# S4 convolution beside a gated FFN: channel halves, channel pairs, and last reads in three parts

## The chip, the cores and the metric

One core of a Trainium2 chip runs the whole program. The metric is the device time of one execution in microseconds; the lower the better. The kernel before the change took 326.91 us (median of 3 runs, 326.82 to 329.02).

## What is computed

The input is `u`, 2048 rows by 640 channels in bf16. Two branches read it and are mixed by a gate per row. The core of the reference:

```python
logdA = exp(log_dt)[:, None] * (A_re + 1j * A_im)            # 640 x 128
K  = einsum("dn,dnl,dn->dl", C, exp(logdA[:, :, None] * l), dt * B).real   # 640 x 2048
a  = irfft(rfft(pad(u.T)) * rfft(pad(K)))[:, :2048].T + u * Dskip
b  = (gelu(u @ w_gate) * (u @ w_up)) @ w_down                # 640 -> 1728 -> 640
g  = sigmoid((u * gate_w).sum(-1))
out = g * a + (1 - g) * b
```

So there is a long convolution per channel with a kernel K that must first be generated from 128 complex states per channel, and a feed-forward network with 1728 hidden units.

## The kernel before, in words

**Generating K.** A time index is split as one of 32 coarse steps times one of 20 fine steps (`X2`), centred at 124, so K at a channel is a product of two small tables summed over the 128 states, which lie on the partitions. `kgen(q)` makes the tables for one half `q` of the channels (320 = `W`): `cs1` (32 coarse steps) and `cs2` (20 fine steps), each with a cosine and a sine plane. ScalarE writes the magnitudes (`exps1`, L599: 32 activations of 320 elements for each half, one for each sign and step; `exps2`, L627: 20 more) and the sines of the phases (L589); VectorE writes the phases (L580, L582, L584) and the products (L613, L614, L619, L631, L637). `contract(h)` then multiplies on TensorE (L650): four neighbouring channels ("quads") share one matmul, with a 128-column stationary tile (32 steps x 4 channels) and 80 moving columns (20 steps x 4 channels), 80 quads by two planes, so 160 matmuls for each half. Only the quarter of the result in which the channels agree is used. Seven evictions (128x960 and one 128x640, L247 or L243) copy it to `kst`, two groups of selecting matmuls (`pick`, L661) take the wanted quarter, and four DMAs write it to DRAM (`dS`). A first row of K (L669, L672) is made in `contract` too.

**Transforms.** The convolution is done in two stages of matmuls with a small matrix (`WA`, then `TB`), through DRAM between the stages. `ua` (L719) is stage A of u: 16 phases, written to `dU`. `gathers(h)` reads rows of `dS` into the tile `Kl` with 18 DMAs, into runs of 16, 16, 32 and 64 neighbouring partitions, and `stageA(h)` (L780) writes the stage-A result for one half to `dKA`, which holds both halves side by side (rows of 640 channels, of which a half fills 640-byte pieces). Stage B is `stageB` (L807): for each of eight blocks `c` of 4 columns, four groups of matmuls over 64x64 tiles, each followed by an eviction. `u_spec(c)` gives the spectrum `U[c]`; `swap` copies `U[c]` with neighbouring partitions exchanged into `Us` (two DMAs). `mix(c)` loads all 640 channels of `dKA`, runs stage B on them, multiplies `U` and `Us` by the result on VectorE (L826, L827: 128x2560 each), does the inverse stage (L834) and writes `dY`. Only four `Us` buffers exist, so the swaps for c = 4 to 7 come between the mixes.

**Finish.** `finish` reads `dY` back in eight tiles (L847, 640 KB each, all 128 partitions, four buffers in a ring), runs two groups of matmuls for each (L854), combines each with the FFN result on VectorE (L859), and writes the output (L863).

**FFN.** `ffn(0)` and `ffn(1)` are two halves of the rows: 14 gate groups (L500, gelu on ScalarE at L504) and 13 up groups (L520, product on VectorE at L524) each. `downs(0)` and `downs(1)` are eight groups each of 28 matmuls (L548) with one eviction (L245 or L249). `downs(0)` must be through before the hidden units of `ffn(1)` take its buffers.

**The order.** Each operation is added as a numbered step. The list `ORDER` holds one number v for each: step v // 20, engine v % 20 // 4 (PE, DVE, ACT, POOL, SP), PSUM bank pair v % 4. `emit` issues the steps in exactly this order, so every engine's queue is written out by hand, and all DMAs go through SP's queue. The durations and ranks given with each step were input of the planner that made the list; they do nothing at run time. The order of TensorE that matters here: two `downs(0)` groups and 8 of the `ua` phases, then the contraction of half 0, the rest of `downs(0)`, `ffn(1)` with the last `ua` phases between, the contraction of half 1 at 182 us, the stage B of u, stage A of K half 1, and from 238 us on the eight `downs(1)` groups laid singly between stage B of K and the inverse stage. The last of them, `down1.7`, stands before the last inverse groups; after those nothing but the finish is left.

Of the kernel before, what the change touches and what calls it, by code (L numbers as in the profile page):

```python
# [8 lines left out]
ALU = mybir.AluOpType  # L9
# [18 lines left out]
    336 1392 652 276 12 296 356 436 616 476 636 948 516 24 376 416 316 456 496 964 556 536 44 596 1468 576 224 676  # L28
    696 64 896 936 856 2740 1448 876 396 984 6316 796 1484 816 916 836 1408 716 736 1544 2981 2836 776 756 1064 1428
    2862 3076 1004 1024 1044 4383 2956 2768 1124 1084 1104 2888 10580 10604 3008 4404 2782 10636 1508 3020 2804 2856  # L30
    1568 1604 2903 3096 248 3044 88 3101 2976 4428 1664 2602 1148 6320 3196 6348 2624 2924 1168 6362 2656 3220 6436
    6388 1524 1188 6416 3128 3463 3316 3248 4444 3142 1584 3556 3488 1628 3261 3216 3164 1204 6440 1688 3336 6483
    3822 3284 6556 6464 6508 1644 3501 1228 3916 6536 3848 3340 3576 1244 1264 4183 1284 3368 3436 3524 1704 6562
    4208 4276 6600 3581 6676 6588 6628 6656 3703 1724 3608 3676 1304 3622 3728 3796 3940 3696 1324 3644 1348 4061
    4036 104 3968 6683 1364 4156 6722 1944 6796 4088 3860 6748 2004 6708 1748 6776 3981 3936 3884 3382 4056 1828
    1764 4004 1788 4223 3456 3404 1868 1804 4300 4296 1908 1844 4244 128 1924 3741 4376 1884 1968 144 6802 3816 6843
    6916 3764 6828 1984 6868 168 6896 4101 2064 2028 4176 4328 6922 2124 6963 7036 6988 6948 4344 2088 7016 184 4124
    2044 7043 208 7082 7068 4460 2184 7156 7108 2148 7136 2104 2164 2208 9464 7161 7203 4488 4742 7276 7188 2224
    7228 7256 9524 2480 4768 2321 2504 2443 2344 2242 2464 2360 2264 2281 2384 2403 2304 7322 2424 9728 7280 4661
    7396 7304 7344 9768 9744 7376 9808 2523 9784 2560 4684 4502 2588 2544 9848 9824 2716 2736 9408 2696 9864 2676  # L40
    7401 4524 7440 4703 7516 7424 9888 7464 8276 8296 8236 9448 9904 7496 8316 8436 8336 4542 4724 8456 8536 8576
    9388 8416 8356 8396 8496 8476 8556 7521 4564 7560 9428 8256 4583 7636 7584 8376 8516 7544 7616 9488 4622 4604
    9548 9584 7680 7641 4648 9504 4783 7756 7668 7708 7736 4902 4808 4876 9644 5021 9608 4996 9564 7760 5116 7803
    7876 7824 7788 9668 9924 5260 7856 5048 4823 5356 9984 4928 7921 4896 7948 4844 7882 7996 7908 4941 5288 9684
    7976 5142 5016 4964 10008 8003 5236 8040 9624 5061 8116 8068 5136 10104 8028 5300 9948 8096 5383 5376 5324 5168
    10044 8160 5476 5408 8122 8188 5503 5084 8148 8216 9964 5420 5528 5596 9704 10068 5742 10024 5496 5444 8621
    10128 5836 8583 10164 5180 8608 11176 11356 8648 5623 10144 5256 5768 8676 5204 5861 5716 5648 10084 10188 5782
    5956 5540 5804 5856 5888 11536 10204 8723 5616 8682 5564 8708 10221 8748 10262 8776 10244 10300 10284 10343
    10324 10381 10364 8822 10404 8780 8848 10423 8808 10462 8876 10444 11221 11260 10488 11244 11183 11288 11302
    11716 11204 11328 11541 11360 11568 11384 11402 12636 11663 11428 12616 8881 11684 8920 8908 11582 8944 10503  # L50
    11608 11621 10524 10540 11648 12076 8976 5902 10568 12696 12716 10656 10716 10676 11721 11763 5924 11800 11748
    10696 5976 11828 11841 11784 12256 11442 11868 11480 11896 11504 11468 12203 12161 12736 12228 12184 12756 12082
    12120 12656 12108 9023 12144 12676 8981 9048 5982 9004 9076 6080 13076 6008 13036 13056 13116 13096 6163 12976
    6108 13016 12996 12956 12936 12261 12816 12342 6188 12380 12284 12896 12916 12368 12404 12023 12776 12301 12048
    12856 6122 12324 12836 12876 12796 6076 11900 11943 6144 11981 11928 12436 11968 9080 12004 9122 9108 6203 9144
    9176 5661 6224 13120 5684 5736 13162 13148 13363 13188 13260 13384 13321 13288 13222 13216 13344 12443 13248
    12480 12468 12504 12562 13316 9181 13416 12588 12523 9204 6020 12548 13422 6044 13461 13448 13523 13548 13562
    13484 6240 13588 13516 13616 13663 6268 11052 13621 13684 9222 9248 13644 9276 13763 6284 13722 13716 13788
# [11 lines left out]
    17124 17276 17436 17296 17576 17716 17481 17443 17504 17996 17464 17302 17340 17556 17324 17536 17364 17856  # L70
    17581 17623 17396 17604 17416 17644 18136 17722 17760 17744 17676 18276 17784 17696 18041 18003 18064 17816
    17836 18024 18116 17862 18096 17900 17884 17924 17956 18141 17976 18183 18164 18204 18282 18236 18320 18256
    18304 18344 18396 18376
""".split()]


# [64 lines left out]
def kernel(  # L141
# [90 lines left out]
    def evac(n, p, dst, src, r=(), w=(), rank=3.0, act=True, dve=True, scale=None, **k):  # L232
        e = {}
        if act:
            e["ACT"] = an(n)
# [722 lines left out]
```

## Time and profile before

| | us | share of the span |
|---|---|---|
| median of 3 runs | 326.91 | |
| the profiled execution, its own time | 327.61 | |
| its span, first to last instruction | 325.8 | |
| PE (matmuls) busy | 266.1 | 82% |
| PEld (weight loads) busy | 146.7 | 45% |
| DVE (VectorE) busy | 246.3 | 76% |
| ACT (ScalarE) busy | 223.6 | 69% |
| mean granted TensorE clock | 0.922 of full | |

How to read it: an engine's "busy" is the time in which at least one of its instructions ran; weight loads run beside matmuls. A "group" is all instructions of one line, engine and shape, with its busy time and the mean time of one. The "chain of work" goes back from the last instruction, at each step to what released it. A "window" row gives, for a stretch of the span, its length, then the busy time and count for PE, PEld, DVE, ACT and POOL, then the granted clock, the busy share of the 16 DMA engines and the GB/s moved.

### The profile page before, as it was taken

Reading aid. Unit: us, or ns where it says so; the run is one execution under the profiler, and the core shown is the slowest. Engines: PE = TensorE matmul, PEld = TensorE weight load, DVE = VectorE, ACT = ScalarE, POOL = GpSimd, SP = SyncE. Lnnn points to the kernel's source line nnn. Section 1 sums busy time; section 2 is a strip of 40 time slices with the busy share of each in tenths; the row PEclk is TensorE's granted clock in tenths of the full one; section 3 lists DMA queues with packets and bytes.
Section 4 is the critical chain, followed back from the end, with each engine's and each line's share of the span. In section 5 each row is a group of like instructions: output and inputs, shape, how many; then the busy total and the mean of one; then the engine's idle time right before and its main releaser. Section 6 shows DMA issues by size and latency. Waiting matters only on the chain.

```text
span 325.8 us, 5490 instructions
## 1 busy us (share of the span) xinstructions
PE 266.1 (82%) x2112; PEld 146.7 (45%) x2126; DVE 246.3 (76%) x332; ACT 223.6 (69%) x307; POOL 5.3 (2%) x18
## 2 busy tenths in 40 slices
PE   0799999897796999979899987985998889993452
PEld 0254444443366677534344743432465456551220
DVE  4687999999999963799996977254363899982464
ACT  4998997699995599998989576525471386671000
POOL 3000000000000000000000000000110000000000
PEclk9989999999797999999999997999899799998555
DMA  6993344332321144433437659979366569934997
GB/s 171 394 331 104 121 140 125 100 103 81 125 76 42 62 123 130 143 123 120 141 100 240 188 192 291 341 163 260 115 204 221 181 240 330 344 141 163 368 353 245
DMA packets 47519, 60.57 MB, mean 186 GB/s; under 512 B 4419, under 2 KB 41862, under 8 KB 47494
## 3 DMA queue, kind: packets, MB, share of 16 engines
q1 hardware_dynamic: 47494, 60.23, 57.3%
q8 instruction: 16, 0.26, 0.3%
q14 instruction: 9, 0.07, 0.1%
HBM read 35.80 MB, written 19.17 MB: 169 GB/s over the span
## 4 chain that ended last, share of the span: by engine, by line
PE 36%; ACT 22%; DVE 18%; DMA 15%; issue 5%; SPq 3%; DVEq 0%; ACTq 0%
PE ps L548 13%; PE ps L520 8%; PE ps L500 7%; ACT arena L243 6%; ACT arena L589 5%; DVE arena L247 5%; DMA dKA<-arena 4%; ACT arena L599 4%; DMA arena<-dY 3%; DMA arena<-dU 3%; ACT arena L504 3%; DMA arena<-dKA 2%; DVE arena L859 2%; PE ps L650 2%; PE ps L807 2%
## 5 line engine op out<-in xcount | busy, mean ns | idle before, releaser
L243 ACT CAST arena<-ps 128x640 bf16<-128x640 f32 x111 | 70.6, 702 | 38.1 <-PE ps L807 15.7
L500 PE MATMUL ps<-arena 128*128 128x512 bf16 x276 | 66.5, 392 | 13.0 <-DMA arena<-in_u_T_dram 9.2
L247 DVE CAST arena<-ps 128x640 bf16<-128x640 f32 (+2 forms) x67 | 56.2, 881 | 20.1 <-PE ps L807 10.4
L520 PE MATMUL ps<-arena 128*128 128x512 bf16 x250 | 63.1, 401 | 4.2 <-DVE arena L524 1.9
L548 PE MATMUL ps<-arena 128*128 128x320 bf16 x448 | 65.0, 305 | 1.0 <-DVE arena L247 0.5
L548 PEld LDWEIGHTS <-arena 128*128 128x128 bf16 x448 | 44.5, 100 | 20.6 <-issue 2.1
L500 PEld LDWEIGHTS <-arena 128*128 128x128 bf16 x280 | 28.0, 100 | 47.9 <-issue 14.1
L520 PEld LDWEIGHTS <-arena 128*128 128x128 bf16 x260 | 26.5, 103 | 37.2 <-issue 9.3
L589 ACT ACTIVATE arena<-arena 128x2560 bf16<-128x2560 int16 x18 | 41.6, 2334 | 0.4 <-DVE arena L637 0.3
L524 DVE TENSOR_TENSOR arena<-ps,arena 128x1024 bf16<-128x1024 f32 x26 | 31.6, 1218 | 13.1 <-PE ps L520 12.9
L504 ACT ACTIVATE arena<-ps 128x1024 bf16<-128x1024 f32 (+1 forms) x28 | 27.7, 1023 | 9.4 <-PE ps L500 9.2
L807 PE MATMUL ps<-arena 64*64 64x320 bf16 x256 | 16.9, 325 | 9.0 <-DMA arena<-dKA 2.8
L599 ACT ACTIVATE arena<-arena 128x320 bf16<-128x320 f32 x64 | 23.3, 455 | 1.0 <-DVE arena L451 1.0
L854 PE MATMUL ps<-arena 128*64 128x320 bf16 x64 | 10.2, 474 | 14.5 <-DMA arena<-dY 14.5
L859 DVE SCALAR_TENSOR_TENSOR arena<-ps,g_f,arena 128x640 bf16<-128x640 f32 x16 | 13.0, 878 | 11.9 <-PE ps L854 11.9
L249 DVE TENSOR_SCALAR arena<-ps,omg 128x640 bf16<-128x640 f32 x10 | 8.8, 883 | 14.9 <-PE ps L548 14.9
L627 ACT ACTIVATE arena<-arena 128x320 bf16<-128x320 f32 x40 | 14.8, 455 | 5.9 <-PE ps L650 5.9
L582 DVE SCALAR_TENSOR_TENSOR arena<-arena 128x320 int32<-128x320 f32 x40 | 16.9, 483 | 0.8 <-ACT arena L589 0.7
L650 PE MATMUL ps<-arena 128*128 128x80 bf16 x320 | 13.5, 212 | 3.8 <-DVE arena L637 2.8
L807 PEld LDWEIGHTS <-arena 64*64 64x64 bf16 x256 | 8.2, 107 | 17.7 <-issue 9.7
L650 PEld LDWEIGHTS <-arena 128*128 128x128 bf16 x320 | 13.3, 107 | 4.6 <-DVE arena L637 3.5
L780 PE MATMUL ps<-arena 128*128 128x320 bf16 x64 | 12.1, 308 | 4.1 <-DMA arena<-dS 2.3
(93 smaller groups left out, 240.8 us busy)
## 6 DMA issues: line engine op xcount, KB each, us to landing
arena<-in_w_gu_dram SPq DMA_DIRECT2D x52, 160.0 KB, 2.2
dU<-arena SPq DMA_DIRECT2D x16, 320.0 KB, 2.3
arena<-dU SPq DMA_DIRECT2D x8, 640.0 KB, 4.7
dKA<-arena SPq DMA_DIRECT2D x16, 320.0 KB, 4.2
arena<-arena SPq DMA_DIRECT2D x16, 320.0 KB, 4.3
arena<-dKA SPq DMA_DIRECT2D x8, 640.0 KB, 6.0
dY<-arena SPq DMA_DIRECT2D x8, 640.0 KB, 6.1
arena<-dY SPq DMA_DIRECT2D x8, 640.0 KB, 5.6
```

The lines of the kernel that those rows point to most:

```text
L243: nc.scalar.copy(out=dst, in_=src(b))
L247: nc.vector.tensor_copy(out=dst, in_=src(b))
L500: nc.tensor.matmul(ps[:, k + j, :], lhsT=Wg[w][:, kt, :], rhs=xT[2 * grp + j][:, kt, :], start=(kt == 0), stop=(kt == NKT - 1))
L504: add({"ACT": an(1024)}, lambda s: nc.scalar.activation(out=HTall[0:p, :, f, :], in_=ps[0:p, plan.bank(g):plan.bank(g) + 2, :], func=ACT.G ...
L520: nc.tensor.matmul(ps[:, k + j, :], lhsT=Wu[w][:, kt, :], rhs=xT[2 * grp + j][:, kt, :], start=(kt == 0), stop=(kt == NKT - 1))
L524: add({"DVE": v1(1024)}, lambda s: nc.vector.tensor_tensor(out=HTall[:, :, f, :], in0=ps[:, plan.bank(u):plan.bank(u) + 2, :], in1=HTall[: ...
L548: nc.tensor.matmul(ps[:, k + h, 0:W], lhsT=HTq[q][:, f, 128 * j:128 * j + 128], rhs=Wd[f][:, W * h:W * h + W], start=(f == 0), stop=(f == ...
L589: ac(an(8 * W), lambda: nc.scalar.activation(out=t[:], in_=ph.bitcast(I16)[:, :, :, 0:32:2], func=ACT.Sin, scale=SIN_SCALE), r=[f"ph{k}"], ...
L599: nc.scalar.activation(out=cs1[:, 1, :, 4 * s:4 * s + 4], in_=quads(aT[:, ds]), func=ACT.Exp, scale=float(sg * (4 + 8 * i)))
L650: nc.tensor.matmul(ps[:, k + i // g, 80 * (i % g):80 * (i % g) + 80], lhsT=cs1[:, x, k0 + i, :], rhs=cs2[:, x, k0 + i, :], start=(x == 0), ...
L807: nc.tensor.matmul(ps[64 * y:64 * y + 64, k + x, 0:W], lhsT=TB[64 * x:64 * x + 64, 0, :], rhs=t[64 * x:64 * x + 64, 2 * a + y, HV[h]], sta ...
L859: add({"DVE": v1(D)}, lambda s, p=p, ph=ph, z=z: nc.vector.scalar_tensor_tensor(out=z, in0=ps[:, plan.bank(p):plan.bank(p) + 2, 0:W], scal ...
```

## The change

Five things are changed together, and the whole order of issue is a new list (952 steps in place of 920).

1. **Channel pairs.** `contract` takes two channels at a time: a 64-column stationary tile (32 steps x 2) and 40 moving columns (20 x 2), 160 pairs by two planes, so 320 matmuls for each half in place of 160. Pairs of the lower and the upper 80 go to PSUM partitions 0 to 63 and 64 to 127. The evictions are three of 128x960 and one of 128x320 for each half in place of seven. All tables have runs of 2 neighbouring channels in place of 4.
2. **Exps of both signs.** A negated copy `aN` of the decay rates is laid beside them, and one activation of 640 elements writes the steps of both signs: 16 in place of 32 for each half.
3. **Products by half.** `dKA` and the products are split by channel half: the load, stage B and products of half 0 (`product(0, c)`) come before stage A of half 1 is done; half 1 follows with the inverse (`product(1, c)`, `inverse`). Loads are 320 KB in 640-byte pieces, writes are 2,560-byte pieces. There are eight `Us` buffers, and the swap follows each `u_spec`.
4. **Rows spread.** The rows of `u` and K are permuted so that the gathers write every 8th, 4th or 2nd partition. About 25 more operations on one column prepare the index tables (`rows`, `last_rows`).
5. **Last reads in three parts.** `dY` is three tensors (blocks c = 0 to 3; 4 and 5; 6 and 7). Each of the eight tiles, which now have a buffer each, is read by three DMAs into every 2nd, 4th and 4th partition.

In the new list TensorE does three `downs(0)` groups and eleven `ua` phases before the contraction of half 0. After the last inverse groups (block c = 5, whose last K stage comes late) stand `down1.5` and `down1.6`, then the finish. SP has the eight reads of blocks 0 to 3 before the writes of blocks 6, 7 and 5, then reads of blocks 6 and 7, then mostly those of 4 and 5, then the outputs.

```diff
-    cs1 = at(O_CS1, [128, 2, 80, 128], BF16, "cs1")
+    cs1 = at(O_CS1, [128, 2, 160, 64], BF16, "cs1")
...
     def exps1(q, i0, n):
...
         def go():
             for i in range(i0, i0 + n):
-                for s, sg in ((15 - i, -1), (16 + i, 1)):
-                    nc.scalar.activation(out=cs1[:, 1, :, 4 * s:4 * s + 4], in_=quads(aT[:, ds]), func=ACT.Exp, scale=float(sg * (4 + 8 * i)))
+                out = c5[:, 1, 15 - i:17 + i:2 * i + 1] if d < 0 else c5[:, 1, 16 + i:(14 - i if i < 15 else None):-2 * i - 1]
+                nc.scalar.activation(out=out, in_=ab, func=ACT.Exp, scale=float(4 + 8 * i))
...
     def contract(h):
-        for k0 in range(0, 80, 12):
-            n = min(12, 80 - k0)
+        for k0 in range(0, 80, 24):
+            n = min(24, 80 - k0)
...
                 for i in range(n):
                     for x in range(2):
-                        nc.tensor.matmul(ps[:, k + i // g, 80 * (i % g):80 * (i % g) + 80], lhsT=cs1[:, x, k0 + i, :],
-                                         rhs=cs2[:, x, k0 + i, :], start=(x == 0), stop=(x == 1))
+                        for y in range(2):
+                            nc.tensor.matmul(ps[64 * y:64 * y + 64, k + i // g, 40 * (i % g):40 * (i % g) + 40],
+                                             lhsT=cs1[:, x, 80 * y + k0 + i, :], rhs=cs2[:, x, 80 * y + k0 + i, :], start=(x == 0), stop=(x == 1))
...
     def kgen(q):
+        ve(v2(W), lambda: nc.vector.tensor_scalar(out=aN[q][:], in0=aT[:, W * q:W * q + W], scalar1=-1.0, scalar2=None, op0=ALU.mult),
+           r=["aT"], w=[f"aN{q}"], rank=RKQ[q] + P["e1"])
...
+        def rows_of(m0):
+            return {0: slice(0, 128, 8), 16: slice(4, 128, 8), 32: slice(2, 128, 4), 64: slice(1, 128, 2)}[m0]
...
-            dst = Kl[m0:m1, phs, :]
+            dst = Kl[rows_of(m0), phs, :]
...
+    def product(h, u, us, kb, bi, c, UK, keys, R):
         (U, un_), (Us, sn), (t, tn) = u, us, kb
+        ks = stageB(loadB(dKA[h][:], W, keys, bi, c, R), (0,), t, tn, R)
+        for x, kx in zip((U, Us), UK):
+            ve(v2(W * CS), lambda x=x: nc.vector.tensor_tensor(out=x[:, :, HV[h]], in0=x[:, :, HV[h]], in1=t, op=ALU.mult), r=ks,
+               w=[k for k in kx if k[2] == h], rank=R - .1)
...
-    def finish(keys, rings, R):
-        for g in range(8):
-            t, nm = rings[g % len(rings)]
-            dma(640, lambda t=t, g=g: nc.sync.dma_start(out=t, in_=dY[:, 4 * g:4 * g + 4, :]), r=keys, w=[nm], rank=R, run=5120)
+    def finish(tiles, R):
+        for q, (p0, st, cs) in enumerate(((0, 2, (0, 1, 2, 3)), (1, 4, (4, 5)), (3, 4, (6, 7)))):
+            for g, (t, nm) in enumerate(tiles):
+                dma(640 // st, lambda t=t, g=g, q=q, p0=p0, st=st: nc.sync.dma_start(out=t[p0:128:st], in_=dY[q][:, 4 * g:4 * g + 4, :]),
+                    r=[("dY", c) for c in cs], w=[(nm, q)], rank=R + P["F0"] * (2 - q), run=5120)
...
+    uk = [u_spec(U[c], Us[c], bi, c, P["U1"]) for c in range(6)]
+    for c in range(6):
+        product(0, U[c], Us[c], kb[c % 4], bh, c, uk[c], keys[0], P["C0"])
+    keys[1] = stageA(1, Kl1, blocks(O_CS1 + 97280, 4, 2560, 3, "ar", W), 2, P["A1"])
+    uk += [u_spec(U[c], Us[c], bi, c, P["U2"]) for c in range(6, 8)]
+    for c in range(6, 8):
+        product(0, U[c], Us[c], kb[c % 4], bh, c, uk[c], keys[0], P["C0"])
...
     for c in range(8):
-        if c >= 4:
-            swap(U[c], Us[c % 4], uk[c], P["U1"])
-        ys.append(mix(U[c], Us[c % 4], kb[c % 4], bi, c, uk[c], keys, P["C1"]))
+        product(1, U[c], Us[c], kb[c % 4], bh, c, uk[c], keys[1], P["C1"])
+        inverse(U[c], Us[c], yb[c % 3], c, uk[c], P["C1"])
```

## The prediction, made before the result was known

> **What bounds the kernel now.** I first read the page's strip of 40 slices (8.1 us each), to see which engine is full where. Rows: busy tenths of each engine, then the granted clock.
>
> ```profile
> PE   0799999897796999979899987985998889993452
> DVE  4687999999999963799996977254363899982464
> ACT  4998997699995599998989576525471386671000
> PEclk9989999999797999999999997999899799998555
> ```
>
> No engine is full all the way: VectorE and ScalarE are from 40 to 100 us and again from 135 to 182, TensorE from 100 to 135 and nearly so at the end, and the last 29 us have none. So I cut the span at the places where the limit changes and asked for the windows.
>
> ```profile
> 40.00:100.00 60.00, 51.98 (x251) 25.59 (x253) 58.45 (x73) 55.23 (x64) 0.00 (x0) 0.94 0.33 102
> 100.00:135.00 35.00, 34.06 (x363) 25.97 (x365) 25.28 (x36) 27.65 (x59) 0.00 (x0) 0.95 0.35 103
> 135.00:182.00 47.00, 42.65 (x199) 19.53 (x201) 42.84 (x57) 44.18 (x38) 0.00 (x0) 1.00 0.47 146
> 190.00:222.00 32.00, 25.94 (x201) 11.73 (x203) 17.09 (x21) 16.58 (x25) 0.00 (x0) 0.95 0.83 252
> 222.00:255.00 33.00, 26.65 (x193) 15.46 (x195) 15.69 (x19) 15.85 (x24) 2.09 (x2) 0.94 0.64 196
> 255.00:297.00 42.00, 37.82 (x488) 24.22 (x487) 37.53 (x36) 26.70 (x44) 0.00 (x0) 0.97 0.74 251
> 297.00:326.00 29.00, 10.22 (x64) 4.35 (x64) 13.04 (x16) 0.00 (x0) 0.00 (x0) 0.53 0.81 294
> ```
>
> From 40 to 100 VectorE is busy 58.45 of 60 us; from 100 to 135 TensorE 34.06 of 35. From 190 to 255 no engine is full: TensorE idles 6.1 + 6.3 = 12.4 us while K half 1 goes through DRAM (its waits there are on `dS`, `dU` and `dKA`). The chain of work shows how it ends (start, length, what).
>
> ```profile
> 297.05 3.20 DMA dY<-arena
> ...
> 300.74 3.89 DMA arena<-dY
> ...
> 304.67 0.76 PE ps L854 x3
> ...
> 312.38 7.01 DMA arena<-dY
> ```
>
> The last inverse matmul ends at 296.0 (294.44 + 1.58 in the timeline), then write and read of `dY` until 304.67 with TensorE idle for 8.64 us, then eight tiles, of which the last waits for a read until 319.4.
>
> **The change, part by part.** The sum is made against the profiled execution: 327.6 us, of which 325.8 are span.
>
> *The end.* From 296.0 to 325.8 are 29.8 us. In the new order `down1.5` and `down1.6` follow the last inverse groups: 2 x 3.96 = 7.9 us (28 matmuls of L548 in 3.96). Beside them runs the same round trip: eviction 1.0, write 3.2, issue 0.5, and a 160 KB read at 2.2 (what such loads of `u_nat` took) = 6.9, so it is covered. The other reads have been issued before or run beside VectorE: sixteen at some 0.5 us each on SP are 8 us, less than the 13 that VectorE needs. Then 0.9 to the first L859, 16 of them (0.80 to 0.84 each, ten in 8.01) 13.2, and 3.9 from the last one (321.9) to the end: 7.9 + 0.9 + 13.2 + 3.9 = 25.9. **-3.9 us.**
>
> *Those two downs leave the stretch before.* There TensorE is busy 37.82 of 42 us, and 7.9 us of its work go. The ends are 0 (VectorE, 37.53 of 42, becomes the limit) and -7.9. I take **-6**, near the TensorE end, since half of the products also leave this stretch.
>
> *Products by half.* K stage B of half 0, 16 products and then inverse groups of half 0 are ready while half 1 is on its way through `dKA`. Of the 12.4 idle us, the waits on `dKA` are 2.8 and those on `dU` 2.3 in the list of waits, 2.3 more are on `dS`, which no half-0 product removes from the path of half 1. Ends 0 and -8; I take **-4**, what `dKA` and half of `dU` make. Two products of 128x1280 (0.82 by L613) replace one of 128x2560 (1.48), 32 x 0.82 - 16 x 1.48 = +2.5 us on VectorE, of which half falls where VectorE is under half busy: 0, at most +2.5. The 24 added DMAs cost SP about 0.48 us each (median issue of the `dY` reads), 11.5 us in a stretch where SP mostly waits: 0, at most +3, one K load being late on each of few occasions.
>
> *Channel pairs on TensorE.* 320 matmuls of 80 columns become 640 of 40. The price before is set by the weight loads, which never pause (columns: PE busy, PEld busy, clock; then the same from the timeline for 64x64 tiles).
>
> ```profile
> 100.30:104.00 3.70, 3.64 (x60) 3.65 (x61) 0.56 0.25 93
> 104.00:108.00 4.00, 3.84 (x104) 3.71 (x101) 0.98 0.00 0
> 294.44 0.81 PEld L834 LDWEIGHTS <-arena 64*64 64x64 bf16 x25 [0.26 <-issue]
> ```
>
> One pair of load and matmul took 3.71 / 101 = 37 ns at full clock and 61 ns at 0.56. Half 0 took 7.48 us and half 1 6.05, together 13.5. A 128x64 tile with 40 columns is not in the trace. The nearest rows are 64x64 loads, four tiles at once: 25 in 0.81 us, (0.81 - 0.11) / 24 = 29 ns, and 8 in 0.24, 20 ns. The ends are 20 ns (640 x 0.020 = 12.8, -0.7) and 61 (39.0, +25.5); two tiles at once lie between one at 37 and four at 20 to 29, so I take 29: 18.6 - 13.5 = **+5.1**, on the path both times, since TensorE is full after half 0, and everything left waits for half 1.
>
> [...] No row here has a 128x64 load at full clock; the 128x64 loads of L854 took 164 ns at half clock, no less than the 150 of 128-column loads near 8 us (L500, where five 512-column matmuls took 2.29 us, about half the pace of ten in 2.16 later).
>
> *VectorE and ScalarE around the K tables.* Gone: 12 evictions of 128x960 (1.15) and 2 of 128x640 (0.8), 15.4 us; new: 6 of 1.15 and 2 of 128x320 (0.48, by L672), 7.9: -7.5. ScalarE: 64 activations take 23.3 busy, 363 ns apart (32 in 11.62); 32 of 640 elements at about 0.74 - 0.09 = 0.65 apart (0.74 by L471, less the overlap of 455 and 363) are 20.7: -2.6. Added on VectorE: two `aN` (0.32 each, by L580) and some 27 one-column operations (0.08 to 0.22): 3 to 6 us, most of them before 13 us, where VectorE is idle 7.3 of 20. But more evictions are queued ahead of the first contraction (three more `ua` phases and a third down, about 5 us on ScalarE at 0.7 each and 2 on VectorE), and that stretch is full. Runs of 2 channels in place of 4: if the products then ran at the pace of the evictions (128x960 in 1.15, so 128x1280 in about 1.5 in place of 0.82), 26 of them (L613, L631) would add 17 us, the phases (L580 from 0.32 to 0.48) 5 more. The trace has no such runs; the same operation takes the same time a channel with runs of 4 (0.82 for 1280) as contiguous (1.48 for 2560), so I take no change. Together **-2**, ends -5 and +22.
>
> *Rows spread.* All TensorE waits on `dS` reads are 3.5 us (2.3 and 1.2, which overlap); 18 gathers are issued as before at 0.4 to 0.6 us each on SP, so at most -2.3; taken as 0.
>
> Sum: -3.9 - 6 - 4 + 5.1 - 2 = -10.8, so 327.6 - 10.8 = **317 us**. The median of the runs shown lies 0.7 below the profiled execution; I leave that inside the rounding.
>
> **Rivals.**
>
> *The weight loads of the pairs set the time.* At 61 ns, the pace at the low clock, the contraction costs +25.5; with the other terms (-15.9) that is 337 us, slower. The break-even is 640p = 13.5 + 15.9, p = 46 ns. For it: loads are already what never pauses in L650, and there will be twice as many. Against it: the 8 selecting loads (128x32, L661) are through within 0.14 us at 0.09 each, so loads into different columns can run together.
>
> *The idle time only moves.* If VectorE holds the stretch from 255 to 297 and half 1 still goes the same way through DRAM, only the end remains: 327.6 - 3.9 + 5.1 = 329, no change that counts. For it: VectorE 37.53 of 42 there. Against: ScalarE is at 26.7 and takes evictions too.
>
> *More than I count.* Pairs at 20 ns, all of the downs' 7.9, 8 of the 12.4, -5 at the tables: 302 by the ends; I put this case at 308.
>
> *The halves of a 64-column pair don't run together, or runs of 2 are slow on VectorE* (+22 in place of -2, so 341): the change then does not do what it says. It ends where the first rival ends and is counted with it.
>
> **How the numbers follow.** A measurement of this kernel tells about 1% from no change, 3.3 us: below 323.6 is faster, above 330.2 slower. The forecast (311 to 323.6) has 0.50, the larger gain 0.15, so faster 0.65; idle time that moves 0.15, same; the slow pairs or slow short runs 0.20, slower. The range goes from 306, which takes in most of the larger gain, to 335, near the price of the rival at 58 ns; it leaves out some 0.15, mostly above.
>
> **What would show it.** L650: 640 matmuls with 64 columns; 160 of them in about 4.6 us if I am right, over 7.5 if the rival is. Evictions behind them: 8 in place of 14. The stretch 190 to 255: TensorE idle of 8 us or less, with L807 of half 0 before the last L780. The end: two downs after the last L834, no TensorE gap over 2 us before L854, and L859 sixteen in a row in some 13.5 us. L613 and L631 at 0.82 us; if they show 1.4, the forecast is wrong at the tables. It is wrong at the end if L854 waits for `dY` late, because SP's sixteen reads are issued one behind another.

## The result, and the profile after

The changed kernel takes **367.05 us** (median of 4 runs, 366.18 to 367.94), beside 327.16 for the kernel before in the same comparison: a ratio of 1.121, 95% interval 1.116 to 1.126. That is 40 us slower; 317 had been forecast, and the range ended at 335. The profiled execution has a span of 365.4 us (before 325.8). All line numbers below are those of the changed kernel, unless another kernel is named.

The strip of 40 slices of the changed kernel (9.1 us each; the rows are busy tenths of TensorE, VectorE and ScalarE, then the granted clock) shows where to look first:

```profile
PE   0930199999887989944579997778495889899562
DVE  4960069999999989602399992554256689996285
ACT  2222889999998969637078893444424596862000
PEclk9975579999998999986869999899987899999965
```

There are two holes that the kernel before doesn't have: TensorE stands still from about 21 to 44 us and VectorE with it, and all three engines are thin from about 155 to 183 us. At the end the hole of the kernel before is gone, but the end is no shorter. The windows of the changed kernel (length, then busy time and count of TensorE, weight loads, VectorE, ScalarE and GpSimd, then the granted clock, the busy share of the DMA engines and GB/s) put numbers to it:

```profile
20.00:40.00 20.00, 1.15 (x46) 1.15 (x44) 3.82 (x9) 7.12 (x11) 0.00 (x0) 0.55 0.37 112
40.00:100.00 60.00, 52.09 (x230) 23.42 (x235) 49.61 (x65) 57.30 (x70) 0.00 (x0) 0.92 0.36 109
...
135.00:182.00 47.00, 33.66 (x202) 18.84 (x200) 21.98 (x28) 27.84 (x44) 0.00 (x0) 0.89 0.24 68
...
300.00:334.00 34.00, 32.03 (x418) 20.72 (x420) 30.12 (x40) 21.88 (x34) 1.04 (x1) 1.00 0.83 270
334.00:366.00 32.00, 17.83 (x137) 10.44 (x136) 16.61 (x20) 0.69 (x1) 0.00 (x0) 0.75 0.80 246
```

From 20 to 40 us TensorE works 1.15 us; in the kernel before it worked 19.32 in the same window. From 135 to 182 no engine is near full, where before VectorE, ScalarE and TensorE all had 42 to 44 of 47. The list of waits of the changed kernel (who waited <- for what: us in all, times, longest) names the two causes, each in several rows:

```profile
PE ps L549 <- ACT arena L533: 24.4, 2, 22.7
...
ACT arena L632 <- DMA arena<-in_B_w_down_dram: 16.5, 3, 5.9
...
DVE arena L611 <- DMA arena<-dS: 13.3, 1, 13.3
...
PE ps L761 <- DMA arena<-in_u_nat_dram: 11.3, 2, 6.6
...
ACT L618 <- DVE arena L613: 10.1, 1, 10.1
...
ACT arena L632 <- DMA arena<-in_w_gu_dram: 8.3, 1, 8.3
ACT arena L618 <- DMA arena<-dS: 8.2, 1, 8.2
...
DVE arena L646 <- DMA arena<-dS: 6.4, 1, 6.4
```

First cause: the exps (L632) wait 24.8 us for loads of weights (`in_w_gu`, `in_B_w_down`), which they don't read; gelu (L533) stands behind them on ScalarE, and TensorE waits 22.7 us for gelu. Second cause: the phases, sines and products of the K tables of half 1 (L611, L618, L646) wait for `dS`, that is for the gathers of half 0, which write the tile `Kl` and touch none of these tables. On SP it goes the other way: the loads of `w_down` (L474) wait 15.2 us for the exps. The timeline of ScalarE shows the exps of half 0 in four groups, each behind a load (start, length, what, and in brackets the idle time before and what ended it); before, 32 of them ran in one piece from 6.76 to 18.38 us:

```profile
13.71 2.71 ACT L632 ACTIVATE arena<-arena 128x640 bf16<-128x640 f32 x4 [8.33 <-DMA arena<-in_w_gu_dram]
22.33 2.68 ACT L632 ACTIVATE arena<-arena 128x640 bf16<-128x640 f32 x4 [5.91 <-DMA arena<-in_B_w_down_dram]
29.94 2.65 ACT L632 ACTIVATE arena<-arena 128x640 bf16<-128x640 f32 x4 [4.93 <-DMA arena<-in_B_w_down_dram]
38.21 2.65 ACT L632 ACTIVATE arena<-arena 128x640 bf16<-128x640 f32 x4 [5.62 <-DMA arena<-in_B_w_down_dram]
```

The operations themselves cost what had been counted, or less, but for 1.2 us of exps (L660). The groups of the changed kernel (busy us and mean ns of one, then idle time before them):

```profile
L873 DVE TENSOR_TENSOR arena<-arena 128x1280 bf16<-128x1280 bf16 x32 | 24.3, 819 | 0.1
L632 ACT ACTIVATE arena<-arena 128x640 bf16<-128x640 f32 x32 | 21.3, 743 | 26.2 <-DMA arena<-in_B_w_down_dram 16.5 <-DMA arena<-in_w_gu_dram 8.3 <-PE ps L696 1.4
...
L660 ACT ACTIVATE arena<-arena 128x320 bf16<-128x320 f32 x40 | 16.0, 509 | 0.0
...
L696 PE MATMUL ps<-arena 128*64 128x40 bf16 x640 | 12.0, 191 | 3.7 <-issue 3.7
```

The 640 matmuls of the channel pairs are busy 12.0 us; the 320 of the quads were busy 13.5, half 0 of them at a granted clock of 0.77. The end, in the timeline of TensorE of the changed kernel (the last inverse matmuls, two downs, then the finish):

```profile
333.93 0.74 PE L884 MATMUL ps<-arena 64*64 64x320 bf16 x16
334.60 7.78 PE L577 MATMUL ps<-arena 128*128 128x320 bf16 x56
346.29 1.15 PE L907 MATMUL ps<-arena 128*64 128x320 bf16 x8 [3.90 <-DMA arena<-dY]
```

And in its chain of work (start, length, what):

```profile
330.12 0.59 SPq L898
331.45 8.79 DMA dY<-arena
340.81 0.59 SPq L898
...
349.09 3.42 DMA arena<-dY
```

The two downs do stand in the place of the 8.64 us of idle time. But a write of `dY` (the second of the last three) takes 8.79 us behind eight reads of 320 KB that SP issued before it, then SP issues the sixteen last reads at 0.63 us each (10.02 us), and the finish starts 3.90 us after the downs. The read whose landing (at 346.24) frees the first matmul of the finish is the sixth of the sixteen, issued at 343.35.

### The profile page after: what moved, and what is told of

Same layout as the page of the kernel before. It is cut to its first block, busy times and chain, and to the rows that moved or that the text cites. A ratio compares the mean times of both kernels' runs of the same rounds, so it can differ in the third digit from the quotient of the medians.

```text
span 365.4 us, 6216 instructions
## 1 busy us (share of the span) xinstructions
PE 270.6 (74%) x2432; PEld 146.7 (40%) x2446; DVE 247.6 (68%) x374; ACT 220.9 (60%) x272; POOL 5.2 (1%) x17
## 4 chain that ended last, share of the span: by engine, by line
PE 31%; DMA 20%; DVE 16%; ACT 15%; SPq 11%; issue 5%; DVEq 0%; ACTq 0%
PE ps L577 9%; PE ps L549 7%; PE ps L529 7%; ACT arena L632 6%; DVE arena L248 4%; DMA arena<-dS 3%; SPq L898 3%; PE ps L696 3%; SPq L789 3%; ACT arena L660 3%; DMA arena<-in_B_w_down_dram 3%; DVE arena L553 2%; DMA dY<-arena 2%; ACT arena L244 2%; DMA arena<-arena 2%
## 5 line engine op out<-in xcount | busy, mean ns | idle before, releaser
L244 ACT CAST arena<-ps 128x640 bf16<-128x640 f32 (+2 forms) x107 | 68.5, 699 | 38.3 <-PE ps L825 11.5
L549 PE MATMUL ps<-arena 128*128 128x512 bf16 x253 | 64.0, 405 | 25.7 <-ACT arena L533 24.4
L529 PE MATMUL ps<-arena 128*128 128x512 bf16 x273 | 69.0, 404 | 14.0 <-DMA arena<-in_u_T_dram 9.8
L248 DVE CAST arena<-ps 128x640 bf16<-128x640 f32 (+2 forms) x65 | 52.7, 847 | 32.5 <-PE ps L696 8.6
L577 PE MATMUL ps<-arena 128*128 128x320 bf16 x448 | 66.9, 310 | 2.4 <-DVE arena L553 2.0
L577 PEld LDWEIGHTS <-arena 128*128 128x128 bf16 x448 | 44.7, 101 | 23.2 <-DVE arena L553 2.4
L549 PEld LDWEIGHTS <-arena 128*128 128x128 bf16 x260 | 26.7, 103 | 59.8 <-issue 34.3
L529 PEld LDWEIGHTS <-arena 128*128 128x128 bf16 x280 | 28.8, 103 | 49.8 <-issue 17.3
L618 ACT ACTIVATE arena<-arena 128x2560 bf16<-128x2560 int16 x18 | 41.8, 2335 | 10.1 <-DMA arena<-dS 8.2
L632 ACT ACTIVATE arena<-arena 128x640 bf16<-128x640 f32 x32 | 21.3, 743 | 26.2 <-DMA arena<-in_B_w_down_dram 16.5
L533 ACT ACTIVATE arena<-ps 128x1024 bf16<-128x1024 f32 (+1 forms) x28 | 27.5, 1023 | 8.6 <-PE ps L529 8.5
L852 PE MATMUL ps<-arena 64*64 64x320 bf16 x256 | 18.1, 323 | 12.6 <-DVE arena L248 4.1
L611 DVE SCALAR_TENSOR_TENSOR arena<-arena 128x320 int32<-128x320 f32 x40 | 16.9, 487 | 13.3 <-DMA arena<-dS 13.3
L761 PE MATMUL ps<-arena 128*128 128x320 bf16 x64 | 13.0, 314 | 16.2 <-DMA arena<-in_u_nat_dram 11.3
L873 DVE TENSOR_TENSOR arena<-arena 128x1280 bf16<-128x1280 bf16 x32 | 24.3, 819 | 0.1
L646 DVE TENSOR_TENSOR arena<-arena 128x1280 bf16<-128x1280 bf16 x16 | 13.1, 821 | 6.8 <-DMA arena<-dS 6.4
L912 DVE SCALAR_TENSOR_TENSOR arena<-ps,g_f,arena 128x640 bf16<-128x640 f32 x16 | 13.2, 879 | 4.9 <-PE ps L907 4.7
L825 PE MATMUL ps<-arena 128*128 128x320 bf16 x64 | 11.9, 303 | 5.8 <-DMA arena<-dS 4.7
L660 ACT ACTIVATE arena<-arena 128x320 bf16<-128x320 f32 x40 | 16.0, 509 | 0.0
L618 ACT ACT_TABLE_LOAD x6 | 7.7, 1283 | 13.5 <-DVE arena L613 10.1
```

Source lines behind the costliest of these rows:

```text
L244: nc.scalar.copy(out=dst, in_=src(b))
L248: nc.vector.tensor_copy(out=dst, in_=src(b))
L529: nc.tensor.matmul(ps[:, k + j, :], lhsT=Wg[w][:, kt, :], rhs=xT[2 * grp + j][:, kt, :], start=(kt == 0), stop=(kt == NKT - 1))
L533: add({"ACT": an(1024) + 60}, lambda s: nc.scalar.activation(out=HTall[0:p, :, f, :], in_=ps[0:p, plan.bank(g):plan.bank(g) + 2, :], func= ...
L549: nc.tensor.matmul(ps[:, k + j, :], lhsT=Wu[w][:, kt, :], rhs=xT[2 * grp + j][:, kt, :], start=(kt == 0), stop=(kt == NKT - 1))
L577: nc.tensor.matmul(ps[:, k + h, 0:W], lhsT=HTq[q][:, f, 128 * j:128 * j + 128], rhs=Wd[f][:, W * h:W * h + W], start=(f == 0), stop=(f == ...
```

## The experiments

Four places in the timelines of TensorE cut the span into stages: the first matmul of the contraction of half 0, the last one of half 1, the last inverse matmul, the end. This table is the measure for what follows (us; for before 100.36, 187.83 + 1.59, 294.44 + 1.58, 325.8, and the others from the same rows; "both repairs" and "gathers first" are kernels below, the second with two profiles, `e6_gathers_first` and `e10_gathers_again`).

| stage | before | after | both repairs | gathers first |
|---|---|---|---|---|
| to the first contraction | 100.4 | 126.8 | 100.4 | 100.5, 100.2 |
| from there to the end of the second | 89.1 | 102.7 | 82.1 | 81.4, 81.5 |
| to the last inverse matmul | 106.6 | 105.2 | 104.0 | 104.0, 100.7 |
| to the end | 29.8 | 30.7 | 31.5 | 28.8, 29.2 |

The theory was that the program orders instructions on the one big memory tile by the address ranges that their operands span, and that two of the new operands span things that they don't touch: the exps read the rates and their negation with one operand, and the negation of half 0 lies 36,864 bytes per partition in front, with the down, gate and up weights, `TB` and `WA` between; the gathers write every 8th, 4th or 2nd partition. The rivals: these operations are slow in themselves, or the loss belongs to the pairs or to the new order of the list. The first three kernels are the two repairs, alone and together. Where a kernel ran once, its difference (19 us and more) is far outside the 1 to 5 us by which runs of one kernel differ.

**The negated rates beside the rates** (label `e1_neg_beside`):

```diff
-    O_NEG = (O_TT + 7680, O_A + 8960)
-    aN = [at(o, [N, W], FP32, f"aN{q}") for q, o in enumerate(O_NEG)]
+    O_NEG = (O_A - 1280, O_A + 8960)
+    aN = [arena[:, O_NEG[0] // 2:(O_NEG[0] + 1280) // 2].bitcast(FP32), at(O_NEG[1], [N, W], FP32, "aN1")]
```

> The changed kernel with one thing moved: the negated decay rates of channel half 0 lie directly in front of the rates that they belong to (1,280 bytes, in a stretch of WA that is written much later), and no longer 50 KB away with the FFN weights between the two. Theory A: the activation that reads both signs reads two rows far apart, and the program's ordering takes the whole stretch between them as read, so it waits for each weight load into that stretch (24.8 us of waits on loads that it does not use), and the loads wait for it. Then the exps end near 18 us in place of 40.9, the 22.7 us gap of TensorE before L549 goes, and the time falls from 367 by 17 to 25 us, to 342 to 350. Rival, the exps only wait for data they need or the gap is bound by the late loads of u and of the gate weights: less than 5 us gained. Rival, the order list has put everything later anyway: the gap at 20 to 43 us goes but the time stays above 358.

Measured: 342.33 us (one run), 24.7 below the changed kernel. The timeline of ScalarE of this kernel:

```profile
6.78 10.39 ACT L632 ACTIVATE arena<-arena 128x640 bf16<-128x640 f32 x16 [1.41 <-DVE arena L722]
```

The same sixteen activations now run in one piece and wait for the operation that makes the negation, no load. They are 0.65 us apart, as the prediction had put them, and 1.2 us shorter than the 32 before (11.62). So neither the length of the activation nor reading two runs at once was the price; where the second run lies was.

**The gathers into neighbouring partitions** (label `e2_rows_together`; the negation stays far off):

```diff
-            return {0: slice(0, 128, 8), 16: slice(4, 128, 8), 32: slice(2, 128, 4), 64: slice(1, 128, 2)}[m0]
+            return {0: slice(0, 16), 16: slice(16, 32), 32: slice(32, 64), 64: slice(64, 128)}[m0]
...
-        "u_nat": u.reshape(128, 16, D)[rows],
+        "u_nat": u.reshape(128, 16, D),
```

`rows` shrinks to one copy, and the index table `tM` gets its step of 16 per partition back.

> The changed kernel with the rows of u and K in their old places: the gathers write runs of neighbouring partitions (0 to 15, 16 to 31, 32 to 63, 64 to 127) and no longer every 8th, 4th or 2nd. Theory B: a write to every n-th partition is taken by the program's ordering as a write to far more of the on-chip memory than it touches, so the gathers wait for the table work of half 1 and that work waits for the gathers (L611 13.3, L618 8.2, L646 6.4, L609 3.5 us on reads of dS in the profile after). Then these waits fall below 3 us in all, TensorE is busy over 40 of the 47 us from the first gather on, and the time falls by 10 to 25 us, to 342 to 357. [...] Rival, the waits are for buffers really shared: they stay.

Measured: 347.58 us (one run), 19.5 below the changed kernel. The window that had been thin, in this kernel:

```profile
135.00:182.00 47.00, 44.59 (x275) 25.11 (x274) 40.86 (x52) 43.86 (x57) 0.00 (x0) 1.00 0.42 122
```

All three engines are full again there, TensorE with 44.59 us in place of 33.66.

**Both** (label `e3_both`):

> Both of the moves above in one kernel. If A and B are independent and are the whole loss, the rest of the change is what the prediction summed, with the contraction now measured (12.0 us of L696 in place of the 18.6 assumed, 13.5 before): 327 - 15.9 - 1.5, so 306 to 318 us, faster than before. If the two moves gain singly but the new order of issue is itself worse, 327 or more. If A and B share one path, the gain over the changed kernel is about that of the larger one alone, 342 to 347.

Measured: 320.05 us (4 runs, 319.09 to 321.27), 2 us above the range expected; ratio to the kernel before 0.977, 0.969 to 0.985. The two repairs give 24.7 and 19.5 alone and 47.0 together, so they hardly share anything, and what is left of the change is faster than the kernel before by some 1.5 to 3%. By the table the first is 26.4 us of the first stage, the second 20.6 of the second stage. Each alone moves only its own stage: the two stages take 100.7 and 102.4 us with the first repair, 127.8 and 81.7 with the second. The timeline of TensorE of this kernel (line numbers 9 lower):

```profile
100.36 4.47 PE L687 MATMUL ps<-arena 128*64 128x40 bf16 x255 [0.96 <-DVE arena L661]
...
218.25 0.69 PE L816 MATMUL ps<-arena 128*128 128x320 bf16 x2 [5.63 <-DMA arena<-dS]
...
286.36 7.78 PE L568 MATMUL ps<-arena 128*128 128x320 bf16 x56
298.56 3.27 PE L898 MATMUL ps<-arena 128*64 128x320 bf16 x24 [4.42 <-DMA arena<-dY]
```

255 pairs follow each other 17.5 ns apart (4.47 / 255), at a granted clock of 1.00. Two stalls are left that the forecast had not at this size: 5.63 us for the gathers of half 1 and 4.42 for `dY`.

**The last reads from neighbouring partitions too** (label `e4_all_together`). The range theory might have put the reads of the finish under the same suspicion, as they write every 2nd or 4th partition:

```diff
-        for q, (p0, st, cs) in enumerate(((0, 2, (0, 1, 2, 3)), (1, 4, (4, 5)), (3, 4, (6, 7)))):
+        for q, (p0, st, cs) in enumerate(((0, 64, (0, 1, 2, 3)), (64, 96, (4, 5)), (96, 128, (6, 7)))):
...
-                dma(640 // st, lambda t=t, g=g, q=q, p0=p0, st=st: nc.sync.dma_start(out=t[p0:128:st], in_=dY[q][:, 4 * g:4 * g + 4, :]),
+                dma(5 * (st - p0), lambda t=t, g=g, q=q, p0=p0, st=st: nc.sync.dma_start(out=t[p0:st], in_=dY[q][:, 4 * g:4 * g + 4, :]),
```

The index table of the finish (`last_rows`) goes back with them.

> As the kernel with both moves, and the last reads of dY also into neighbouring partitions (0 to 63, 64 to 95, 96 to 127 in place of every 2nd and 4th); the amounts, the number of reads and the order are the same. Theory B holds for these reads too: they wait for more than they need, and so does what follows; then this is 2 to 8 us faster than the kernel with both moves, with TensorE's waits on dY (6.2 us after) below 3. [...]

Measured: 324.27 us (10 runs, 323.02 to 327.34), 4.2 above the kernel with both repairs; ratio to before 0.991, 0.986 to 0.996. Here the suspicion falls and the spreading earns its place. The DMA issues from 270 us on in this kernel (KB each, median us to landing):

```profile
arena<-dY SPq DMA_DIRECT2D x8, 320.0 KB, 8.6
arena<-dY SPq DMA_DIRECT2D x16, 160.0 KB, 5.3
```

And the same in the kernel with both repairs:

```profile
arena<-dY SPq DMA_DIRECT2D x8, 320.0 KB, 5.7
arena<-dY SPq DMA_DIRECT2D x16, 160.0 KB, 3.1
```

TensorE waits 11.1 us for `dY` with neighbouring partitions and 6.7 with spread ones. Why reads into neighbouring partitions land later, no run shows. The 640 KB writes of `dY` that share the queues land late with the reads, 10.2 us in place of 5.5.

**Each cause alone on the kernel before.** That the two repairs bring the time back doesn't show that the two parts would cost as much without the rest. Two kernels put one part each into the kernel before, with its own order, quads and products. The exps of half 0 with the far negation (label `e7_signs_alone`):

```diff
+    aN = at(O_TT + 7680, [N, W], FP32, "aN")
...
-                for s, sg in ((15 - i, -1), (16 + i, 1)):
-                    nc.scalar.activation(out=cs1[:, 1, :, 4 * s:4 * s + 4], in_=quads(aT[:, ds]), func=ACT.Exp, scale=float(sg * (4 + 8 * i)))
+                nc.scalar.activation(out=c5[:, 1, 15 - i:17 + i:2 * i + 1], in_=ab, func=ACT.Exp, scale=float(4 + 8 * i))
```

> The kernel before with one part alone: in half 0 one activation writes the steps of both signs, 16 in place of 32, and the negated rates lie where the change puts them, about 46 KB per partition in front of the rates, with the weight tiles between. Half 1, the channel quads, the order and all else are as before. Theory (the operand's range covers the tiles between, and the program makes the exps wait for the weight loads that land there and the loads for the exps): the exps of half 0, through at 18.4 us in the kernel before, end at 25 to 40 us, TensorE has a gap of several us before 45 us, and the time is 8 to 25 us longer than before, 335 to 352. Rival (one activation over two far apart runs, or over both signs, is itself slow, and waits have no part): the exps would show 1.3 us or more each and no waits on loads, 16 x 0.6 = +10 us on ScalarE alone.

Measured: 351.44 us (one run; before 326.40, median of 7), +25.0. (The distance is 36,736 bytes here and 36,864 in the changed kernel; the 46 KB of this expectation and the 50 KB of the first were miscounted.) From its timeline of ScalarE, two of four such groups:

```profile
13.75 2.62 ACT L608 ACTIVATE arena<-arena 128x640 bf16<-128x640 f32 x4 [8.09 <-DMA arena<-in_w_gu_dram]
21.18 2.61 ACT L608 ACTIVATE arena<-arena 128x640 bf16<-128x640 f32 x4 [4.81 <-DMA arena<-in_B_w_down_dram]
```

The exps end at 40.6 us and TensorE waits 21.9 for gelu, with quads and in the old order. The spread rows alone (label `e8_rows_alone`), with the gathers and `u_nat` as in the change and `rows` called ahead of the masks:

```diff
-            dst = Kl[m0:m1, phs, :]
+            dst = Kl[rows_of(m0), phs, :]
...
-        "u_nat": u.reshape(128, 16, D),
+        "u_nat": u.reshape(128, 16, D)[rows],
```

> The kernel before with one part alone: the rows of u and K are permuted and the gathers write every 8th, 4th or 2nd partition, with the one-column operations that this needs put in front of the masks. All else, the order too, is as before. Theory (the program takes such a write as touching far more than it does, and puts gathers and table work of half 1, which share nothing, one behind the other): waits of VectorE and ScalarE on the gathers appear between 120 and 190 us that the kernel before does not have, and the time is 10 to 20 us longer than before, 337 to 347. Rival (the price belongs to the new order of the whole list, and the kernel before, with its own order, takes the spread rows without loss or with the gain of faster landing): within 3 us of 327.

Measured: 351.27 us (one run), +24.9, more than the upper end of what was expected. Its list of waits from 115 to 190 us:

```profile
DVE arena L596 <- ACT arena L605: 21.6, 1, 21.6
ACT arena L615 <- DMA arena<-dS: 16.2, 3, 5.7
...
PE ps L735 <- DMA arena<-in_u_nat_dram: 13.9, 1, 13.9
...
DVE arena L647 <- DMA arena<-dS: 5.4, 1, 5.4
```

The exps (L615) and a table product (L647) of half 1 wait for gathers of half 0; phases (L596) wait for sines behind those exps, and TensorE for rows of u that are queued on SP behind the gathers. In the same window of the kernel before, the longest wait of an exp, a phase or a table product is 1.6 us. The new order of the list is not the cause; the spread is. How far the program takes such a write to reach was not measured. The two largest gathers (280 KB) land in 3.2 us here and in 4.0 in the kernel before, those of 10 to 70 KB in medians of 2.3 to 4.0 here and 2.6 to 4.3 before; but spread gathers are issued with the waits between them, so what faster landing alone is worth stays open.

**The end in another order** (label `e5_reads_by_tile`). On top of both repairs, SP's list at the end: three reads of blocks 0 to 3, the writes of blocks 6 and 7, one read, the write of block 5, two reads, and then the rest tile by tile.

> The kernel of the experiment with both repairs (negated copy beside the rates, gathers into neighbouring partitions; 320.05 us), with SP's list at the end rewritten: of the eight 320 KB reads of blocks 0 to 3, three go ahead of the last three writes, one between them and four behind, and the 160 KB reads follow tile by tile in the order in which TensorE takes the tiles. Theory (at the end, the write of block 5 stands behind eight reads in the DMA queues and the reads behind each other on SP): the last write lands some 3 us earlier, TensorE waits for dY at most 3 us in all in place of 6.7, and the time is 3 to 6 us lower, 314 to 317. Rival (the end is limited by the bytes that must move, 2.56 MB of late reads and writes whatever their order): within 1 us of 320. What would speak against both: more than 322, if the reads of blocks 0 to 3 that now stand behind the writes come late for the last tiles.

Measured: 320.25 us (4 runs, 319.24 to 321.59; ratio 0.980, 0.974 to 0.986): no gain. In the profile the last stage is 2.1 us shorter (29.4 against 31.5) and TensorE waits 4.2 us for `dY` in place of 6.7, the larger part of it now in the middle of the finish; the medians don't show it. The theory is half right on the waits and wrong on the time.

**The gathers ahead of the swaps** (label `e6_gathers_first`). Swaps write every 2nd partition, so here too a wait without need was suspected: four swap DMAs of blocks 0 and 3, which stood on SP in front of or among the gathers of half 1, go behind them.

> The same, and four swaps (of blocks 0 and 3) that stand on SP between the writes of dS of half 1 and its gathers, or among the gathers, are put behind all 18 gathers. In the kernel with both repairs the first gather of half 1 is issued at 209.8 us, 10 us after the last write of dS, and waits 5.5 us for the swaps, whose writes go to every 2nd partition of a buffer that the gathers don't touch; TensorE then waits 5.6 us for dS. Theory (the wait on swaps is one more that the program orders without need): the gathers start some 4 to 5 us earlier, the wait of TensorE shrinks to under 2 us, and the time is 2 to 4 us below that of the kernel with the new end alone. Rival (what comes free there is lost again, because the later products and inverse groups wait for VectorE and for the round trip of half 1): within 1 us of it.

Measured: 316.56 us (4 runs, 315.26 to 316.82; ratio 0.968, 0.963 to 0.973), 3.7 below its neighbour in the same comparison. In the kernel with both repairs SP's list of waits has the gathers (L788) behind the swaps, whose buffers end where that of the gathers begins:

```profile
SPq L788 <- DMA arena<-arena: 5.5, 3, 3.5
```

With the gathers first, the first of them is issued at 206.85 us in place of 209.78 (2.29 us after the end of the issue before it), and TensorE in this kernel (line numbers 10 lower) waits 1.77 us for it:

```profile
215.19 0.45 PE L815 MATMUL ps<-arena 128*128 128x320 bf16 x2 [1.77 <-DMA arena<-dS]
```

The wait is of the same kind a third time, in an operation that the kernel before has too. How the 3.7 us come about is less clear: of the 2.6 us between the two profiles (spans of 317.3 and 314.7 us) 0.6 lies in the last stage (29.4 and 28.8). TensorE waits 3.5 us for `dKA` with the gathers first, against 2.1 in the kernel with both repairs, and by the table the stage to the last inverse matmul is no shorter in this profile (104.0) than there. Where the rest comes from was not taken apart.

**Reads in twos** (labels `e9_reads_in_twos`, and `e10_gathers_again` for comparison): one DMA reads blocks 4 and 5, or 6 and 7, for two neighbouring tiles.

```diff
+                    elif g % 2 == 0:
+                        o = (O_CS1 + (0 if g < 4 else 40960) + 5120 * (g % 4)) // 2
+                        nc.sync.dma_start(out=arena[p0:128:st, o:o + 5120].rearrange("p (n w) -> p n w", w=D), in_=dY[q][:, 4 * g:4 * g + 8, :])
```

> The kernel with both repairs, the new end and the gathers ahead of the swaps (316.56 us), with the last reads of dY (blocks 4 to 7) issued for two tiles at a time: 8 reads of 320 KB in place of 16 of 160 KB, the bytes and the order otherwise as before. There SP issues the last 20 reads from 287.4 to 300.7 us, 0.66 us apart, and TensorE waits 4.8 us in all for dY. Theory (the end is held by the issue of the reads on SP): the 12 that are left take some 8 us, TensorE's waits for dY fall under 3 us, and the time is 1 to 3 us lower, 313.5 to 315.5. Rival (it is held by the bytes, the DMA engines being busy 0.8 of the time from 255 us on): the reads are issued further apart, the waits of TensorE stay between 4 and 6 us, and the time is within 1 us of the kernel that runs beside it.

> The kernel with both repairs, the new end and the gathers ahead of the swaps once more, for the comparison on the same chip. 315.5 to 317.5 us if its first figure, 316.56, holds; the theory for the kernel with reads in twos is judged by the difference between the two.

Measured: 315.59 us (6 runs, 313.83 to 318.49; ratio to before 0.966, 0.960 to 0.971) beside 315.95 (313.72 to 317.98; ratio 0.965, 0.960 to 0.970). The waits do what the theory said, 2.8 us in place of 3.7, and then VectorE runs through, as its timeline in the kernel with reads in twos shows:

```profile
295.68 12.76 DVE L908 SCALAR_TENSOR_TENSOR arena<-ps,g_f,arena 128x640 bf16<-128x640 f32 x16 [2.44 <-PE ps L903]
```

The last stage has 27.8 us against 29.2 in the kernel beside it. The times are equal within what six runs can tell. Whether the end is held by issue or by bytes therefore stays open at the size of 1 us.

## Why the prediction was wrong

**Where it failed: two terms that were priced by their instructions alone.** "Rows spread" was taken as 0 because 18 gathers are issued as before. The repair brings 19.5 us, 22.3 with the other repair made (342.33 - 320.05), and the part alone costs 24.9. "VectorE and ScalarE around the K tables" had -2, with ends of -5 and +22, and the +22 were for slow runs of 2 channels; the exps of both signs cost 24.7, 27.5 (347.58 - 320.05) and 25.0. Both operands stood in the diff with their offsets and steps, and what is loaded in between could be read in the layout; the step that failed was to ask only how long an instruction runs and not what the program makes it wait for, and on whose queue the waiting stands. None of the four rivals had such waits in it, so none of them is what happened: the 0.20 given to "slower" stood on slow pairs and slow short runs, and neither was there.

**Channel pairs: sign and size wrong, in the good direction.** Taken at 29 ns, +5.1; measured 12.0 against 13.5 busy, -1.5, with eight evictions as said, and 17.5 ns from one to the next with both repairs, below the lower end of 20 that had come from 64x64 loads. 160 matmuls had been put at 4.6 us; 255 took 4.47. The -1.5 is not a clean price, as each kernel has one stretch at a low clock: half 0 of the quads at 0.77 (7.48 us), the last 112 pairs at 0.58 (2.90 us). The quads of half 1 are busy 6.05 us at a granted clock of 1.00 in the kernel before, and those of half 0 take 5.91 in one piece in the kernel with both signs alone (label `e7_signs_alone`); 320 pairs at 16.6 to 17.5 ns (255 in 4.23 and 4.47, both at 1.00) would take 5.3 to 5.6, so the pairs cost little less than the quads did. The rival of the weight loads (61 ns) is refuted.

**Runs of 2 channels: right.** The products of the tables (128x1280) take 0.82 us as before (L646 821 ns, L664 819) and the phases 0.32 (L609 323 ns), so that rival is refuted. The exps into runs of 2 (L660) take 509 ns in place of 455, 1.2 us busy in all, which had not been counted. The activations of both signs have the 0.65 us of the prediction.

**The stretch after the second contraction: too much hoped for.** -6 for the downs and -4 for the products by half were expected to show from 190 to 297; with both repairs that stage is 2.6 us shorter, with the gathers first 2.6 in one profile and 5.9 in the other. "Products by half" was to remove the wait for `dKA` (2.8 us before) and half of that for `dU` (2.3). With both repairs the matmuls of TensorE no longer wait for `dU`, but still 2.1 us for `dKA`, and their wait for `dS`, 2.3 before and left out of the term, has become 5.6; 3.9 of this go when the gathers stand ahead of the swaps. What this stage didn't give, the one before it did: it is 7.0 us shorter, where the terms had +5.1 and -2. Which of the parts (three downs and eleven phases ahead of an equally early contraction, cheaper pairs, fewer evictions) gave how much of it was not taken apart.

**The end: the mechanism right, its cover wrong.** The two downs replace the idle time, and VectorE's sixteen operations take 12.8 to 13.2 us as counted. But 25.9 us had been forecast and 30.7 came: the 3.9 of TensorE's wait, and 1.2 between the sixteen operations. Two terms were too small. The round trip, put at 6.9 us and covered by 7.9, takes longer behind eight reads of 320 KB: the write in the chain has 8.79 us in place of 3.2. And the sixteen reads, put at 8 us beside VectorE, take 10.02 and begin only when that write has landed. The prediction had named this last one as what would make it wrong. With the reads in another order and in twos, 27.8 is left.

**In sum.** The terms, -10.8 together, come near what is left when the needless waits that were found are gone: 320.05 with two repairs, 315.95 and 316.56 with the new end and the gathers first as well, against 317. That is luck: the errors offset each other, and the terms are not met one by one.

## What to carry to other kernels

When an operand becomes strided, or reaches from one buffer to another, list what lies within its whole span and who loads or computes there at that time: each such instruction can become a wait, in both directions and on the queue of whoever issues it (here 24.8 us of exps behind loads of weights, and 15.2 of loads behind exps). Put tiles that one operand reads together next to each other, and keep writes that step over partitions away from stretches in which other engines work in the same memory tile (the spread gathers cost 19.5 to 24.9 us here; the spread last reads, at the end, gained 4.2). A priced list of instructions says what a change can give; the list of waits says whether the program lets it.

## What the runs showed of the hardware

Pairs of a 128x64 weight load and a matmul of 40 columns, into alternating halves of the output partitions, follow each other 16.6 to 17.5 ns apart (255 in 4.23 us in the changed kernel and in 4.47 with both repairs, at a granted clock of 1.00), against 37 for 128x128 loads with 80 columns (101 loads in 3.71 us in the kernel before, at 0.98; 160 matmuls in 5.91 in `e7_signs_alone`). Reads of 320 KB into every 2nd partition land in 5.7 us and into 64 neighbouring ones in 8.6; reads of 160 KB into every 4th in 3.1 and into 32 neighbouring ones in 5.3, at the end of this kernel and in the same order of transfers (medians in `e3_both` and `e4_all_together`). SP issues the spread reads 0.63 to 0.66 us apart in a row (sixteen in 10.01 in `e3_both`, twenty in 13.26 in `e5_reads_by_tile` and `e6_gathers_first`); one issue takes 0.59 in the median in `e3_both`, against 0.48 for the eight reads of 640 KB in the kernel before.
